# Gate's low parts of the first chunk: from GpSimd to VectorE

## The chip, the core and the metric

The kernel runs on one core of a Trainium2 chip. The metric is the time of one execution on the device in microseconds (us). The engines are TensorE (PE in the profile), VectorE (DVE), ScalarE (ACT), GpSimd (POOL) and the queue engine SyncE (SP). Each works through its own instructions in order and waits on semaphores for the others.

## What is computed

Attention in which a query sees the first `n_sink` (4) keys and the `window` (128) keys that end at itself, for 4 batches of 8 heads, 768 positions and head width 64; then, on the 3072 tokens of width 512 that result, a gated layer with a hidden width of 1536:

```
scores = scale * q @ k.T, outside window and sinks -1e9
a = exp(scores - max);  a = a / (sum(a) + 1e-9)
x = (a @ v), heads joined: 3072 x 512
out = ((x @ w_a) * (x @ w_b)) @ w_out
```

## The kernel before

**Tiling.** The tokens are taken in eight chunks (`CHUNKS`): the first has four tiles of 128 tokens, the second two, the others three. For each chunk `moe` runs over j = 0 to 11, the twelve slices of 128 of the hidden width. `half("a", j)` and `half("b", j)` are twelve matmuls each (L813), ScalarE brings a out of PSUM as g (L832), VectorE multiplies b into it (L838), and `project` multiplies the slice by its part of `w_out` (L822), one j later than the slice was made. In the first chunk these tiles are 512 columns wide.

**Split numbers.** Every matmul of this part is three matmuls of float16: each value is a high part and a low part, and low times low is left out. For g the high part gh is a cast on ScalarE (L841). The low part gl is g minus gh (L843), a subtraction of two operands in SBUF. It is done on GpSimd for j = 0 to 9 and on VectorE for j = 10 and 11. g has a single buffer, so that the next j's g (L832) waits until gh and gl of this j are taken; gh and gl have two each.

**Weights.** They come as 64-bit words and are converted once, during the first chunk: `weight_bits` (L352, L354 on VectorE and L353 on ScalarE), `weight_sum` (L361, VectorE), `weight_high` (L367, ScalarE), `weight_low` (L372, VectorE). From the seventh on two weights are converted by one instruction of each kind. The order of the weights is that of their use: w_a and w_b of slice j, then w_out of slice j - 2.

**Attention beside it.** While `moe` works on one chunk, `between` advances the attention of the next by some steps. In the first chunk this attention rounds its keys and queries on ScalarE (L401) and takes their rest on VectorE (L407), not on GpSimd; all its score tiles go through one PSUM bank `s`. A score tile (L530, PE) is read by VectorE (L540), which frees the bank for the next; then come exp (L542, ACT), two small operations (L544, L545, DVE), the division (L553, ACT) and a transpose (L578, PE). At a group's end the sinks' part is added to x (L605 on PE, L607 on VectorE).

**What sets the order.** A scheduler places each engine's instructions by priorities and by its own idea of when they become ready, except where `keep_in_program_order` binds them (the conversions are bound among themselves). L843 is not bound. `run` makes the chunks one after the other and calls `moe`.

Of the kernel before, what the change touches and what calls it, by code (L numbers as in the profile page):

```python
# [18 lines left out]
B, H, S, D = 4, 8, 768, 64  # L19
DM, FF = 512, 1536  # L20
P = 128
# [3 lines left out]
NJ = FF // P  # L25
# [207 lines left out]
class Fast:  # L233
# [562 lines left out]
            xs.append((xh, xl))  # L796
        return xs

    def moe(self, row, nt, xf, between, weights_ahead, last):
        nc = self.nc  # L800
        n = nt * P
        tag = f"{row}"
        xs = self.split_x(xf, nt, tag)
        outs = [self.ps.tile([P, DM], F32, tag=("o0", "o1", "o2", "av")[i], name=f"o{tag}_{i}") for i in range(nt)]

        def half(kind, j):
            wh, wl = self.weight(kind, j)
            ps = self.ps.tile([P, 4 * P], F32, tag=kind, name=f"{kind}{tag}_{j}")
            for kk in range(NK):
                ksl = slice(kk * P, (kk + 1) * P)  # L810
                xh, xl = xs[kk]
                for i, (w, x) in enumerate(((wh, xh), (wh, xl), (wl, xh))):
                    nc.tensor.matmul(ps[:, :n], lhsT=w[:, ksl], rhs=x[:, :n],  # L813
                                     start=kk == 0 and i == 0, stop=kk == NK - 1 and i == 2)
            return ps

        def project(j, gh, gl):
            wh, wl = self.weight("o", j)
            for i in range(nt):
                sl = slice(i * P, (i + 1) * P)  # L820
                for k, (g, w) in enumerate(((gh, wh), (gh, wl), (gl, wh))):
                    nc.tensor.matmul(outs[i], lhsT=g[:, sl], rhs=w,  # L822
                                     start=j == 0 and k == 0, stop=j == NJ - 1 and k == 2)

        prev = None
        for j in range(NJ):
            if last and j == NJ - 2:
                self.good = self.verdict()
            weights_ahead(3 * j)
            pa = half("a", j)  # L830
            g = self.mo.tile([P, max(n, 3 * P)], F32, tag="g", name=f"g{tag}_{j}", bufs=1)
            nc.scalar.activation(g[:, :n], pa[:, :n], AF.Copy, scale=G_UP / (X_UP * W_UP) ** 2)  # L832
            between(3 * j)
            if last and j == NJ - 1:
                self.tc.mark_branch_hint_location("general", hint="LikelyTaken", engines=mybir.ALL_ENGINES)
            weights_ahead(3 * j + 1)
            pb = half("b", j)
            nc.vector.tensor_tensor(g[:, :n], pb[:, :n], g[:, :n], op=ALU.mult)  # L838
            gh = self.mo.tile([P, max(n, 3 * P)], F16, tag="gh", name=f"gh{tag}_{j}")
            gl = self.mo.tile([P, max(n, 3 * P)], F16, tag="gl", name=f"gl{tag}_{j}")  # L840
            nc.scalar.copy(gh[:, :n], g[:, :n])  # L841
            e = nc.gpsimd if j < NJ - 2 else nc.vector
            e.tensor_tensor(gl[:, :n], g[:, :n], gh[:, :n], op=ALU.subtract)  # L843
            between(3 * j + 1)
            weights_ahead(3 * j + 2)
            if prev is not None:
                project(*prev)
            between(3 * j + 2)
            if j >= 2 and self.unsummed:
                o, k = self.unsummed.pop(0)  # L850
                self.sum_rows(o, o, k)
            prev = (j, gh, gl)
        project(*prev)
        down = 1.0 / (G_UP * W_UP)
        scalar = lambda o, ps: nc.scalar.activation(o, ps, AF.Copy, scale=down)
        vector = lambda o, ps: nc.vector.tensor_scalar(o, ps, down, None, op0=ALU.mult)
        os = [self.mo.tile([P, DM], F32, tag="os", name=f"os{tag}_{i}", bufs=4) for i in range(nt)]
        if not last:
            for i in range(nt):
                r = row + i * P  # L860
                scalar(os[i], outs[i])
                nc.scalar.dma_start(self.out[r:r + P, :], os[i])
                self.unsummed.append((os[i], r // P))
            return
        pin = self.tc.keep_in_program_order
        for i in range(nt):
            r = row + i * P
            if i == nt - 1:
                for c, (e, q) in enumerate(((scalar, nc.sync), (vector, nc.scalar))):
                    sl = slice(c * (DM // 2), (c + 1) * (DM // 2))  # L870
                    pin(e(os[i][:, sl], outs[i][:, sl]))
                    pin(q.dma_start(self.out[r:r + P, sl], os[i][:, sl]))
                continue
            pin(scalar(os[i], outs[i]))
            nc.sync.dma_start(self.out[r:r + P, :], os[i])
            if i == 0:
                pin(self.sum_rows(outs[i], os[i], r // P, down))
        for i in range(1, nt):
            sums = self.rows[:, row // P + i:row // P + i + 1]
            if i == nt - 1:  # L880
                pin(self.sum_rows(outs[i], os[i], row // P + i, down))
            else:
                pin(nc.scalar.activation(outs[i], outs[i], AF.Square, scale=down, accum_out=sums))
# [10 lines left out]
    def run(self, scalars, verdict, whole):  # L894
        chunks = CHUNKS
# [4 lines left out]
        def weights_to(n, ahead):  # L900
            wide = range(SINGLE, 2 * PAIRS)
            while loaded[0] < min(n + ahead, len(order)):
                if loaded[0] >= len(order) - 4 and done[0] <= 2 * PAIRS:
                    break
                self.load_weight(loaded[0])
                loaded[0] += 1
            while done[0] < min(n + DELAY, len(order) + DELAY):
                k = done[0]
                done[0] += 1
                singles = lambda d: 0 <= k - d < len(order) and k - d not in wide  # L910
                if singles(3):
                    self.weight_low(k - 3, 1)
                if k % 2 == 0 and k - 2 in wide:
                    self.weight_low(k - 2, 2)
                if singles(2):
                    self.weight_high(k - 2, 1)
                if singles(1):
                    self.weight_sum(k - 1, 1)
                if k % 2 == 1 and k - 1 in wide:
                    self.weight_sum(k - 1, 2)  # L920
                    self.weight_high(k - 1, 2)
                if singles(0):
                    self.weight_bits(k, 1)
                if k % 2 == 0 and k in wide:
                    self.weight_bits(k, 2)
# [5 lines left out]
        b, t0, nt = chunks[0]  # L931

        x = self.wp.tile([P, NK, nt * P], F32, tag=f"w{3 * NJ // 2 - 1}", name="xf0")
        xf = [x[:, i, :] for i in range(NK)]
# [12 lines left out]
        for c, (b, t0, nt) in enumerate(chunks):  # L947
            gen = None
            if c + 1 < len(chunks):
                nb, nt0, nnt = chunks[c + 1]  # L950
                nxf = self.new_xf(c + 1)

                self.banks = ("t", "o2") if nt == 2 else ("t",)
                gen = (self.attention if c else self.attention_in_one_bank)(nb, nt0, nnt, nxf)
                steps = H * nnt + (6 if c else 7)
            taken = [0]

            def between(s):
                if gen is None:
                    return  # L960
                if c == 1 and s == 0:
                    self.join_masks()
                if c:
                    want = min(steps, -(-steps * (s + 1) // (3 * NJ - 3)))
                else:
                    n = HALF * nnt + 2
                    want = 1 if s < BEGIN else max(-(-n * (s + 1 - QUIET) // (MID - QUIET)), 2)
                    if s >= MID:
                        want = min(steps, n - (n - steps) * (s + 1 - MID) // (3 * NJ - 3 - MID))
                while taken[0] < want:  # L970
                    next(gen, None)
                    taken[0] += 1

            def ahead(s):
                weights_to(max(s + AHEAD, done[0] + 1 - DELAY), LOADS)
                if (c, s) in checks:
                    self.check_weight(*order[checks.index((c, s))])
                elif self.unchecked:
                    self.check_weight(None, 0)

            self.moe(b * S + t0 * P, nt, xf, between, ahead, c + 1 == len(chunks))
            if gen is not None:
                for _ in gen:
                    pass
                xf = nxf
# [76 lines left out]
```

## Time and profile before

| | |
|---|---|
| three runs | 731.34, 732.73, 732.94 us, median 732.73 |
| the profiled execution | 734.26 us |
| its span in the profile | 732.5 us |
| TensorE busy in the span | 715.1 us (98%), granted clock 0.999 |
| VectorE, ScalarE, GpSimd busy | 438.2 (60%), 384.5 (52%), 257.6 us (35%) |

The span begins with the first instruction and ends with the last; the 1.8 us between it and the execution's time lie around it. TensorE's 98% are an average: the first 40 us hold the attention of the first chunk, the stretch from about 40 to 160 us its `moe` with the conversion of the weights, and the rest the other seven chunks. An engine's idle time counts only where the time of the whole hangs on it.

### The profile page before, as it was taken

How to read it: one execution, taken by the hardware profiler on the slowest of the kernel's cores; microseconds unless marked ns; L12 is line 12 of the kernel's file. 1: busy time of each engine (PE TensorE's matmuls, PEld its weight loads, DVE VectorE, ACT ScalarE, POOL GpSimd, SP SyncE). 2: the span in 40 equal slices, each digit the busy share in tenths (PEclk: the TensorE clock that was granted, in tenths of full speed). 3: DMA queues.
4: the chain of work that ended last, by engine and by line, in shares of the span. 5: the costliest groups of instructions: out<-in, count | busy, mean ns of one | idle time of the engine just before them, and what ended most of it. 6: DMA issues, size and time to landing. Idle time of an engine off the chain costs nothing.

```text
span 732.5 us, 13093 instructions
## 1 busy us (share of the span) xinstructions
PE 715.1 (98%) x4400; PEld 426.5 (58%) x4400; DVE 438.2 (60%) x1496; ACT 384.5 (52%) x1107; POOL 257.6 (35%) x324
## 2 busy tenths in 40 slices
PE   9999899999999999999999999999999999999996
PEld 4644444457776666566665666556665666655553
DVE  5999999985535665364534555345655545436632
ACT  4957877746655554355543655355553555441112
POOL 1311110356642553254641655225434454101110
PEclk9999999999999999999999999999999999999999
DMA  8988200342221442411221111113333122016411
GB/s 289 345 293 306 68 14 1 108 142 56 63 76 44 123 129 88 141 52 48 62 63 55 46 53 42 65 58 110 105 124 113 59 63 73 4 61 210 155 51 46
DMA packets 43527, 73.35 MB, mean 100 GB/s; under 512 B 4608, under 2 KB 24128, under 8 KB 43456
## 3 DMA queue, kind: packets, MB, share of 16 engines
q1 hardware_dynamic: 40064, 66.70, 28.4%
q10 hardware_dynamic: 3392, 5.77, 2.1%
q8 instruction: 36, 0.59, 0.3%
q14 instruction: 35, 0.29, 0.1%
HBM read 66.16 MB, written 6.29 MB: 99 GB/s over the span
## 4 chain that ended last, share of the span: by engine, by line
PE 83%; DVE 11%; ACT 3%; issue 2%; DMA 0%; ACTq 0%; DVEq 0%
PE o L822 22%; PE b L813 22%; PE a L813 22%; PE s L530 5%; PE av L468 4%; PE t L572 2%; DVE wf L361 2%; DVE w L372 2%; DVE wf L352 2%; DVE wf L354 2%; DVE g L838 1%; PE t L679 1%; PE t L578 1%; PE s_a L644 1%; DVE p L540 1%
## 5 line engine op out<-in xcount | busy, mean ns | idle before, releaser
L813 PEld LDWEIGHTS <-w 128*128 128x128 f16 x2304 | 224.1, 98 | 136.8 <-DVE w L372 0.7
L813 PE MATMUL b<-x,w 128*128 128x384 f16 (+2 forms) x1152 | 205.9, 326 | 0.0
L813 PE MATMUL a<-x,w 128*128 128x384 f16 (+2 forms) x1152 | 205.5, 326 | 0.0
L843 POOL TENSOR_TENSOR gl<-g,gh 128x384 f16<-128x384 f32 (+2 forms) x80 | 76.0, 950 | 301.6 <-ACT gh L841 297.6
L822 PE MATMUL o<-w,gh 128*128 128x512 f16 x576 | 171.8, 379 | 0.7 <-DVE w L372 0.7
L822 PE MATMUL o<-w,gl 128*128 128x512 f16 x288 | 109.0, 379 | 0.1
L841 ACT CAST gh<-g 128x384 f16<-128x384 f32 (+2 forms) x96 | 49.0, 510 | 100.9 <-DVE g L838 98.6
L542 ACT ACTIVATE p<-p,st 128x136 f32<-128x136 f32 (+1 forms) x160 | 66.6, 416 | 52.9 <-DVE st L540 52.1
L838 DVE TENSOR_TENSOR g<-b,g 128x384 f32<-128x384 f32 (+2 forms) x96 | 53.3, 555 | 68.5 <-PE b L813 61.5
L822 PEld LDWEIGHTS <-gh 128*128 128x128 f16 x576 | 55.4, 98 | 51.6 <-ACT gh L841 1.9
L832 ACT ACTIVATE g<-a 128x384 f32<-128x384 f32 (+2 forms) x96 | 46.3, 482 | 68.4 <-PE a L813 59.3
L530 PE MATMUL s<-ks,qh 128*128 128x264 f32 x160 | 66.9, 418 | 5.0 <-DVE st L540 4.6
L550 ACT ACTIVATE p<-p,st 128x128 f32<-128x128 f32 x120 | 48.2, 401 | 40.8 <-DVE st L545 40.6
L544 DVE TENSOR_SCALAR st<-st 128x1 f32<-128x1 f32 x160 | 24.3, 152 | 65.3 <-ACT p L542 64.7
L538 DVE COPY_PREDICATED s<-mg,s 128x128 f32<-128x128 int32 x120 | 35.0, 292 | 41.8 <-PE s L530 41.7
L409 POOL TENSOR_TENSOR ks<-kr,ks 64x400 fp32r<-64x400 f32 (+1 forms) x48 | 56.6, 1178 | 3.8
L403 POOL TENSOR_SCALAR qh<-qr 128x384 fp32r<-128x384 f32 x48 | 24.9, 518 | 83.6 <-PE s L530 66.9
L573 DVE TENSOR_TENSOR pt<-t,tri 128x256 f32<-128x256 f32 x120 | 50.3, 419 | 3.6 <-PE t L572 2.9
L822 PEld LDWEIGHTS <-gl 128*128 128x128 f16 x288 | 28.1, 98 | 36.5 <-DVE gl L843 2.6
L409 POOL TENSOR_TENSOR ql<-qr,qh 128x384 fp32r<-128x384 f32 x48 | 48.6, 1012 | 2.2
L530 PE MATMUL s<-ks,ql 128*128 128x264 f32 x160 | 45.3, 283 | 0.0
L530 PEld LDWEIGHTS s<-ks,qh 128*128 128x128 f32 x160 | 30.3, 189 | 23.7 <-DVE st L540 9.1
(146 smaller groups left out, 902.2 us busy)
## 6 DMA issues: line engine op xcount, KB each, us to landing
qr<-in_qT_dram SPq DMA_DIRECT2D x48, 192.0 KB, 2.4
raw<-in_wa_dram SPq DMA_DIRECT2D x12, 512.0 KB, 6.0
raw<-in_wb_dram SPq DMA_DIRECT2D x12, 512.0 KB, 6.2
raw<-in_wo_dram SPq DMA_DIRECT2D x12, 512.0 KB, 6.9
chk_a<-in_wa_dram SPq DMA_DIRECT2D x24, 256.0 KB, 3.4
chk_b<-in_wb_dram SPq DMA_DIRECT2D x24, 256.0 KB, 3.4
chk_o<-in_wo_dram SPq DMA_DIRECT2D x24, 256.0 KB, 3.3
out_dram<-os ACTq DMA_DIRECT2D x21, 256.0 KB, 2.2
```

The costliest lines, as they stand in the source:

```text
L409: self.nc.gpsimd.tensor_tensor(o, i, high.bitcast(F32), op=ALU.subtract)
L530: mm = nc.tensor.matmul(ps[:, :w], lhsT=q[:, i * P:(i + 1) * P], rhs=ks[:, c0:c0 + w], start=m == 0, stop=m == 1)
L538: nc.vector.copy_predicated(ps[:, KB:], self.up, ps[:, :P])
L542: nc.scalar.activation(p[:, :w], p[:, :w], AF.Exp, bias=st[:, 0:1], scale=-1.0, accum_out=st[:, 1:2])
L550: nc.scalar.mul(p[:, NS:KB], p[:, NS:KB], st[:, 3:4])
L573: nc.vector.tensor_tensor(pt[:, k:k + 2, :], tp[:, 0:1, :].broadcast_to([P, 2, P]), self.tri, op=ALU.mult)
L813: nc.tensor.matmul(ps[:, :n], lhsT=w[:, ksl], rhs=x[:, :n], start=kk == 0 and i == 0, stop=kk == NK - 1 and i == 2)
L822: nc.tensor.matmul(outs[i], lhsT=g[:, sl], rhs=w, start=j == 0 and k == 0, stop=j == NJ - 1 and k == 2)
L832: nc.scalar.activation(g[:, :n], pa[:, :n], AF.Copy, scale=G_UP / (X_UP * W_UP) ** 2)
L838: nc.vector.tensor_tensor(g[:, :n], pb[:, :n], g[:, :n], op=ALU.mult)
L841: nc.scalar.copy(gh[:, :n], g[:, :n])
L843: e.tensor_tensor(gl[:, :n], g[:, :n], gh[:, :n], op=ALU.subtract)
```

## The change

`moe` gets one more argument. It is false for chunk 0 and true for all others, and where it is false gl is taken on VectorE for every j. Ten subtractions of 128x512 go from GpSimd's queue to VectorE's; nothing else is computed in another place.

```
-    def moe(self, row, nt, xf, between, weights_ahead, last):
+    def moe(self, row, nt, xf, between, weights_ahead, last, weights_split):
...
-            e = nc.gpsimd if j < NJ - 2 else nc.vector
+            e = nc.gpsimd if weights_split and j < NJ - 2 else nc.vector
             e.tensor_tensor(gl[:, :n], g[:, :n], gh[:, :n], op=ALU.subtract)
...
-            self.moe(b * S + t0 * P, nt, xf, between, ahead, c + 1 == len(chunks))
+            self.moe(b * S + t0 * P, nt, xf, between, ahead, c + 1 == len(chunks), c > 0)
```

The scheduler also sets other instructions of the first chunk in another order. From the second chunk on the order of all engines is as it was. Three places follow; in a name the number after `g`, `gh` or `gl` is j, and in `p_4_2_0` the numbers are the first tile (4), the head (2) and the tile within (0) of the attention that runs beside.

**Place 1.** VectorE after g of slice 4, before:

```order
L838 TENSOR_TENSOR g_4_979<-b_4_1001,g_4_979 128x512
L407 TENSOR_TENSOR ks_3_4_1021<-kr_2_4_916,ks_3_4_1021 64x400
L372 SCALAR_TENSOR_TENSOR w_896<-wf,w_896 128x1024
L540 ISA p_4_2_0_1031,st_4_2_0_1032<-s_4_2_0_1028,mg 128x264
L540 ISA st_4_2_0_1032 128x1
L352 TENSOR_SCALAR wf<-raw_705 128x1024
```

and now:

```order
L838 TENSOR_TENSOR g_4_979<-b_4_1001,g_4_979 128x512
L407 TENSOR_TENSOR ql_3_4_1023<-qr_3_4_1019,qh_3_4_1022 128x256
L540 ISA p_4_2_0_1031,st_4_2_0_1032<-s_4_2_0_1028,mg 128x264
L540 ISA st_4_2_0_1032 128x1
L372 SCALAR_TENSOR_TENSOR w_896<-wf,w_896 128x1024
L843 TENSOR_TENSOR gl_4_1016<-g_4_979,gh_4_1015 128x512
L352 TENSOR_SCALAR wf<-raw_705 128x1024
```

gl_4 stands three operations behind g_4, and the reading of the score tile (L540) has moved ahead of the conversion L372 and of the rest of the keys ks_3.

**Place 2.** VectorE before the scores of head 6, before:

```order
L407 TENSOR_TENSOR ks_7_4_1380<-kr_6_4_1281,ks_7_4_1380 64x400
L372 SCALAR_TENSOR_TENSOR w_1267<-wf,w_1267 128x1024
L407 TENSOR_TENSOR ql_7_4_1382<-qr_7_4_1378,qh_7_4_1381 128x256
L352 TENSOR_SCALAR wf<-raw_995 128x1024
L540 ISA p_4_6_0_1390,st_4_6_0_1391<-s_4_6_0_1387,mg 128x264
```

and now:

```order
L843 TENSOR_TENSOR gl_7_1375<-g_7_1339,gh_7_1374 128x512
L361 ISA wf<-raw_944,wf 128x2048
L407 TENSOR_TENSOR ks_7_4_1380<-kr_6_4_1281,ks_7_4_1380 64x400
L407 TENSOR_TENSOR ql_7_4_1382<-qr_7_4_1378,qh_7_4_1381 128x256
L540 ISA p_4_6_0_1390,st_4_6_0_1391<-s_4_6_0_1387,mg 128x264
L540 ISA st_4_6_0_1391 128x1
L372 SCALAR_TENSOR_TENSOR w_1267<-wf,w_1267 128x1024
```

Here too L540 now stands ahead of L372, and of L352.

**Place 3.** The sinks' part of the second group, near the end of the first chunk. VectorE before:

```order
L352 TENSOR_SCALAR wf_1597<-raw_1437 128x512
L354 SCALAR_TENSOR_TENSOR wf_1597<-raw_1437,wf_1597 128x512
L372 SCALAR_TENSOR_TENSOR w_1594<-wf_1543,w_1594 128x512
L361 ISA wf_1597<-raw_1437,wf_1597 128x1024
L352 TENSOR_SCALAR wf_1630<-raw_1437 128x512
L607 TENSOR_TENSOR xf_2_620<-t_4_0_0_940,xf_2_620 128x256
```

and now:

```order
L352 TENSOR_SCALAR wf_1597<-raw_1437 128x512
L607 TENSOR_TENSOR xf_2_620<-t_4_0_0_940,xf_2_620 128x256
L354 SCALAR_TENSOR_TENSOR wf_1597<-raw_1437,wf_1597 128x512
L372 SCALAR_TENSOR_TENSOR w_1594<-wf_1543,w_1594 128x512
L361 ISA wf_1597<-raw_1437,wf_1597 128x1024
```

TensorE there, before and then now:

```order
L813 MATMUL a_10_1634<-x_3_631,w_1481 128x512
L605 MATMUL t_4_0_0_940<-sct_4_1_1623,vs_4_4_1108 128x256
L813 LDWEIGHTS w_1540
L813 MATMUL b_10_1655<-x_0_622,w_1540 128x512
```

```order
L813 MATMUL b_10_1655<-x_2_628,w_1540 128x512
L605 MATMUL t_4_0_0_940<-sct_4_1_1623,vs_4_4_1108 128x256
L813 LDWEIGHTS w_1540
L813 MATMUL b_10_1655<-x_2_628,w_1540 128x512
```

The addition L607 has moved ahead of four conversions, and the matmul L605 that it reads from stands eight matmuls later; the second L605, which needs L607's bank, still follows all twelve matmuls of b_10.

## Rows read from the trace of the kernel before

**Rows 1.** Stretches: busy us (instructions) of each engine, clock, DMA share, GB/s.
```profile
0.00:40.00 40.00, 38.49 (x272) 22.60 (x274) 31.02 (x117) 27.42 (x85) 9.51 (x26) 1.00 0.93 324
40.00:160.00 120.00, 110.90 (x573) 53.85 (x570) 113.48 (x199) 83.99 (x183) 25.99 (x23) 1.00 0.36 121
160.00:733.00 573.00, 565.75 (x3561) 350.08 (x3559) 293.75 (x1182) 273.11 (x841) 222.11 (x275) 1.00 0.26 80
```

**Rows 2.** Waits of TensorE, 40 to 160 us: total us, times, longest.
```profile
PE s L530 <- DVE st L540: 4.4, 4, 1.6
PE t L605 <- DVE xf L607: 1.6, 1, 1.6
PE t L578 <- ACT xf L586: 1.4, 2, 1.2
PE o L822 <- DVE w L372: 0.7, 1, 0.7
PE t L578 <- ACT pt L579: 0.6, 1, 0.6
```

**Rows 3.** Waits of TensorE from 160 us to the end.
```profile
PE gp L90 <- DVE good L88: 2.8, 1, 2.8
```

**Rows 4.** GpSimd's timeline, first and last gl: start, duration, [idle before <-releaser].
```profile
47.94 1.48 POOL L843 TENSOR_TENSOR gl<-g,gh 128x512 f16<-128x512 f32 x1 [10.93 <-ACT gh L841]
...
139.59 2.39 POOL L843 TENSOR_TENSOR gl<-g,gh 128x512 f16<-128x512 f32 x1 [9.20 <-ACT gh L841]
143.25 1.65 POOL L403 TENSOR_SCALAR ks<-kr 64x400 fp32r<-64x400 f32 x2 [1.27 <-DMA kr<-in_kT_dram]
```

**Rows 5.** VectorE's timeline, one operation (L361) beside these two, and alone.
```profile
48.32 1.65 DVE L361 CUSTOM_DVE_ANT_0 wf<-raw,wf 128x1024 uint16<-128x1024 uint16 x1
...
131.29 0.69 DVE L361 CUSTOM_DVE_ANT_0 wf<-raw,wf 128x1024 uint16<-128x1024 uint16 x1
...
141.44 1.09 DVE L361 CUSTOM_DVE_ANT_0 wf<-raw,wf 128x1024 uint16<-128x1024 uint16 x1
```

**Rows 6.** VectorE's timeline, gl of slices 10 and 11, and the operation behind.
```profile
151.91 0.98 DVE L843 TENSOR_TENSOR gl<-g,gh 128x512 f16<-128x512 f32 x1
...
156.64 0.69 DVE L843 TENSOR_TENSOR gl<-g,gh 128x512 f16<-128x512 f32 x1 [0.68 <-ACT gh L841]
157.25 1.62 DVE L792 SCALAR_TENSOR_TENSOR x<-xf,x 128x256 f16<-128x256 f32 x4
```

**Rows 7.** TensorE's timeline, four of its waits.
```profile
84.76 0.39 PE L530 MATMUL s<-ks,qh 128*128 128x264 f32 x1 [0.89 <-DVE st L540]
...
108.16 0.44 PE L578 MATMUL t<-ident,p 128*128 128x128 f32 x2 [1.20 <-ACT xf L586]
...
121.70 0.39 PE L530 MATMUL s<-ks,qh 128*128 128x264 f32 x1 [0.93 <-DVE st L540]
...
146.99 0.38 PE L605 MATMUL t<-sct,vs 128*128 128x256 f32 x1 [1.59 <-DVE xf L607]
```

**Rows 8.** ScalarE's timeline, the division ahead of L586.
```profile
107.33 0.52 ACT L553 ACTIVATE p<-p,st 128x264 f32<-128x264 f32 x1 [1.75 <-DVE st L545]
```

**Rows 9.** Groups of VectorE, 46 to 150 us: busy us, mean ns | idle before.
```profile
L372 DVE SCALAR_TENSOR_TENSOR w<-wf,w 128x1024 f16<-128x1024 f32 x11 | 13.4, 1223 | 1.4 <-ACT w L367 1.2
```

**Rows 10.** Timelines of VectorE and ScalarE, g and gh of slices 0 and 9.
```profile
46.51 0.69 DVE L838 TENSOR_TENSOR g<-b,g 128x512 f32<-128x512 f32 x1
47.24 0.62 ACT L841 CAST gh<-g 128x512 f16<-128x512 f32 x1 [1.06 <-DVE g L838]
...
136.94 0.68 DVE L838 TENSOR_TENSOR g<-b,g 128x512 f32<-128x512 f32 x1
138.91 0.60 ACT L841 CAST gh<-g 128x512 f16<-128x512 f32 x1
```

**Rows 11.** The last conversion of a weight (VectorE), and its first use (TensorE).
```profile
152.82 1.48 DVE L372 SCALAR_TENSOR_TENSOR w<-wf,w 128x512 f16<-128x512 f32 x1
157.59 0.59 PE L822 MATMUL o<-w,gh 128*128 128x512 f16 x2
```

## The prediction

> **What bounds the kernel now.** I read the stretches first. From 160 us to the end TensorE is busy 565.75 of the 572.5 us that are left of the span [rows 1], and the only wait of note there is the final check, 2.8 us [rows 3]; the order of these chunks is unchanged, so they should take what they took. The first 40 us hold no gl. What is open is the stretch from 40 to 160 us: TensorE is busy 110.90 of 120 us, so it loses 9.1 us, while VectorE is busy 113.48 of 120 us [rows 1]. The waits say the same from the other side: 4.4 us for the PSUM bank of the scores that VectorE must first read (L540), 1.6 us for L607 on VectorE, 0.7 us for a converted weight, and 2.0 us for ScalarE's copies [rows 2]. In this stretch VectorE is the engine that is late, and 9.1 us is the most that any change here can give back.
>
> **What the change removes.** While GpSimd takes a gl, an operation of VectorE that should begin stands still. The first gl runs from 47.94 to 49.42 [rows 4]; VectorE's L361 begins at 48.32 and takes 1.65 us, where the same operation alone takes 0.69 [rows 5]: 0.96 us lost. The tenth gl holds VectorE less, 1.09 against 0.69 us, 0.40 us [rows 5], and is held up itself, 2.39 us [rows 4]. I found one such operation at each of the ten gl and took its excess over its like beside no GpSimd work: 7.9 us for the ten, from 0.40 to 0.97 us each.
>
> That trace fits a rule of the Trainium skill, "SBUF — State Buffer", section "Who interferes with whom": GpSimd and VectorE share one pair of ports, and where both read SBUF through it, VectorE with two operands as here, whichever comes second is blocked until the first has finished. By that rule the loss would be the whole rest of GpSimd's operation, 49.42 - 48.32 = 1.10 us for the first [rows 4, 5] where its stretching shows 0.96; over ten some 9.3 instead of 7.9 us, and VectorE's balance below would be -3.2 instead of -1.8 us. I take the stretching, which is measured.
>
> **What it adds.** Ten subtractions on VectorE. gl of slices 10 and 11 show the price at this very width: 0.69 us undisturbed, 0.61 us from its start to the next start, and 0.98 us where GpSimd runs beside it [rows 6]. Beside nine of the ten GpSimd will have nothing to do (its next work, the keys of a later chunk, begins at 143.25 [rows 4]), so I take 0.61: 6.1 us for ten, with 9.8 us as the upper end. VectorE's balance is 6.1 - 7.9 = -1.8 us, and +1.9 us at the upper end.
>
> A second rule speaks against the change: "Perfetto Trace Analysis", section "Optimizing Scalar/DVE Operations", says that where VectorE is saturated, offloading work to ScalarE or GpSimd may make sense, though between VectorE and GpSimd it might not help. VectorE is saturated here, so by the first half the move is the wrong way and the 6.1 us come on top; this is a rival below. The stretched operations [rows 5] bear out the second half.
>
> **What it adds as a wait.** gl now stands in VectorE's queue and needs gh from ScalarE; behind it stand conversions, L540 and L607, and behind those TensorE. From the end of g to the end of gh it took 47.86 - 47.20 = 0.66 us at slice 0 and 139.51 - 137.62 = 1.89 us at slice 9 [rows 10], over the ten 13.4 us. The new order puts other work between g and gl: at place 1 a subtraction, L540 and L372, of which L372 alone is 1.22 us [rows 9]. Only for the last three slices is the work between about as short as the lag or a little shorter (at slice 9 two short conversions against 1.89 us). Bounds: nothing, or 1.2 us if ScalarE kept its old order; it takes gh_9 earlier now, so I count nothing.
>
> **Which waits of TensorE go.** VectorE gaining 1.8 us would by itself bring about 1.8 us. But TensorE waits at single points, and the new order moves them too. In order of time:
> - 0.7 us for a weight [rows 2]: the first stall (0.96) is gone and one gl (0.61) stands ahead of it, so 0.35 us.
> - The four waits for the bank make 4.4 us [rows 2]. In the first (1.6 us) L540 falls behind more of VectorE's work than before and I give it nothing. By the second four stalls (3.6 us) have been exchanged for four gl (2.4 us); VectorE is 1.2 us ahead, so TensorE is at most 1.2 us ahead in all. At place 1 L540 passes L372, 1.22 us [rows 9], and the 0.89 us [rows 7] go: 2.1 us so far.
> - 1.20 us behind L586 on ScalarE [rows 7]: L586 queues behind L553, which waits 1.75 us for VectorE's L545 [rows 8], late by a stall. ScalarE now has L586 first. I count 0.5 of it, since the weights then lie close: 2.6 us.
> - 0.93 us at head 6 [rows 7]: at place 2 L540 passes L372 and L352. 0.85 us: about 3.4 us.
> - 1.59 us at L605 [rows 7]: at place 3 L607 passes four conversions, and TensorE has eight matmuls to do before the first L605. All of it: 5.0 us.
>
> The end of the chunk sets a limit of its own: the last weight is ready at 154.30, its matmuls begin at 157.59 [rows 11], 3.3 us later; with VectorE 1.8 us ahead TensorE can be 5.1 us ahead and no more.
>
> So the ends are 1.8 us (VectorE's balance alone) and 5.0 us (every new place pays). Which it is cannot be read from before, as ScalarE is also busy 83.99 of 120 us [rows 1] in its own new order; new small waits are likely. I take the middle, 3.4 us. The profiled execution of 734.26 us would be 730.9; it lies 1.5 us over the median of 732.73, and the same 3.4 us off the median make 729.3 us.
>
> **Rivals.**
> - *No difference.* VectorE gets ahead, but the waits only move: in the new order two readings of score tiles follow each other directly, so VectorE itself waits for TensorE between them, and conversions fall behind where L540 passes them. For it: the exchange is worth only 1.8 us in all. Against: the weights have 3.3 us to spare at the end [rows 11]. A gain of 0 to 1.4 us: about 732.
> - *Slower: VectorE stands at gl for gh.* The place is L843 in VectorE's queue. If ScalarE, with 70% of its time taken [rows 1], brings gh 0.6 us late each time, VectorE loses 6.0 us against the 1.8 won: +4.2 us, 736.9 us. It turns the sign at a mean wait of 0.18 us and is slower by a measurable amount from 0.33 us. Against: the work placed between g and gl.
> - *Slower: relief taken from a saturated engine.* The 6.1 us come on top and the stalls do not come back, because VectorE would have stood there for other reasons. Less the 3.3 us to spare that is +2.8 us, 735.5 us. Against: behind the stretched operations VectorE goes on without idling.
> - *More than forecast.* If the bank waits vanish altogether, up to 6 us: 726.7.
>
> **How the numbers follow.** A measurement of this kernel can tell about 0.2% (1.5 us) from no change, so faster means under 731.3 and slower over 734.2. Forecast (1.8 to 5.0 us off: 727.7 to 730.9) 0.62, more than that 0.06, no difference 0.21, slower by the wait for gh 0.08, by the load 0.03. Faster 0.68, same 0.21, slower 0.11. The range goes from 727.0, a little beyond the forecast's end, to 733.8, which takes in most of the no-difference case.
>
> **What would show it.** VectorE's operations of the first chunk without stretched ones until GpSimd starts on the keys; ten gl on VectorE near 0.69 us, no idle time before them for ACT gh; TensorE's idle time from 40 to 160 us down from 9.1 to about 5.7 us, above all no wait at L605; after that the chunks as long as before. Idle time at gl of over 2 us in all, or TensorE losing more than 8 us in this stretch, would make the prediction wrong.

## The result and the profile after

The changed kernel takes 725.6 us in the median of four runs (724.88 to 726.1) against 732.84 us of the kernel before (731.34 to 734.97). The ratio is 0.9898, with a 95% interval from 0.9872 to 0.9925: 7.2 us less. Forecast were 729.3 us with a range from 727.0 to 733.8, so the direction was right, but the gain is about twice what I expected and lies outside the range.

The stretches of the changed kernel, to be held against [rows 1]. The columns are busy us (instructions) of PE, PE's weight loads, DVE, ACT and POOL, then clock, DMA share, GB/s:

```profile
0.00:40.00 40.00, 38.11 (x300) 22.97 (x301) 33.43 (x121) 28.66 (x88) 9.51 (x26) 1.00 0.95 336
40.00:160.00 120.00, 116.37 (x607) 58.64 (x606) 113.00 (x235) 87.11 (x198) 14.88 (x19) 1.00 0.38 127
160.00:725.00 565.00, 557.11 (x3496) 343.55 (x3494) 287.20 (x1151) 267.84 (x822) 217.82 (x270) 1.00 0.26 79
```

From 40 to 160 us TensorE now loses 3.6 us instead of 9.1. But TensorE also issued 300 matmuls in the first 40 us where it had issued 272, in a stretch without any gl. The fixed windows thus mix two things. A better ruler lies inside the program: the twelve g of the first chunk (L838). Here are the first and the last of them on the timeline of VectorE in the changed kernel:

```profile
43.15 0.69 DVE L838 TENSOR_TENSOR g<-b,g 128x512 f32<-128x512 f32 x1
...
146.82 0.68 DVE L838 TENSOR_TENSOR g<-b,g 128x512 f32<-128x512 f32 x1
```

and the last one of the kernel before, whose first stands in [rows 10] at 46.51:

```profile
155.27 0.69 DVE L838 TENSOR_TENSOR g<-b,g 128x512 f32<-128x512 f32 x1 [0.97 <-PE b L813]
```

This cuts both executions into three. Up to the first g: 46.51 and 43.15 us, 3.36 less. From the first to the last: 108.76 and 103.67, 5.09 less. From there to the end of the span: 577.2 and 577.2. The sum, 8.45 us, is the difference of the two profiled executions, 734.26 - 725.81. So the first chunk gave 5.1 us, the later chunks nothing, and 3.4 us come from a place that the change does not touch.

This ruler is VectorE's. In the kernel before, the last g waited for the last matmul of b_11 and began 0.1 us behind it, as the first g does in both kernels. In the changed kernel these matmuls (the first line here) end at 145.37 us, and the last g begins 1.4 us later, because VectorE is still busy:

```profile
142.62 2.75 PE L813 MATMUL b<-x,w 128*128 128x512 f16 x12
...
155.54 0.39 PE L530 MATMUL s<-ks,qh 128*128 128x264 f32 x1 [0.60 <-DVE st L540]
```

TensorE was thus 6.4 us ahead at this point and gave 1.2 us back behind it, 0.46 at L822 and 0.60 at the L530 shown, both while waiting for VectorE. In the changed kernel VectorE is still the late engine at the end of the chunk.

What VectorE did between these two g, in the kernel before and then in the changed one (columns as above):

```profile
46.50:155.28 108.78, 99.68 (x506) 48.58 (x505) 104.55 (x182) 77.91 (x172) 24.53 (x21) 1.00 0.33 106
```

```profile
43.14:146.83 103.69, 100.66 (x509) 48.97 (x508) 100.96 (x192) 77.89 (x172) 9.19 (x11) 1.00 0.34 114
```

VectorE has exactly ten instructions more (192 against 182), the ten gl, and is busy 3.6 us less. Its idle time fell too, from 4.2 to 2.7 us. 3.6 and 1.5 make the 5.1 us.

The remaining waits of TensorE from 40 to 160 us (total us, times, longest), to be held against [rows 2]:

```profile
PE s L530 <- DVE st L540: 1.9, 2, 1.3
PE o L822 <- DVE w L372: 0.7, 2, 0.5
PE a L813 <- ACT w L367: 0.3, 1, 0.3
PE t L605 <- ACT sct L598: 0.3, 1, 0.3
```

The bank's waits went from 4.4 to 1.9 us (1.25 us in the first chunk, and the new 0.60 us shown above), the 1.59 us at L605 behind L607 is gone, and the 1.2 us behind L586 have no successor. Half of a microsecond at L822 is new, and so are 0.3 us each at L813 and, behind ScalarE, at L605. Of the 9.1 us of waits before, 7.6 us went, and 1.7 us of new ones came. The difference, 5.9 us, is more than the chunk's 5.1, since TensorE also idles 0.4 us longer in pieces too short for this list and loses 0.2 us more at an L530 behind 160 us.

On GpSimd nothing meets VectorE until late; its timeline begins, after the start, with

```profile
119.87 0.24 POOL L292 IOTA col<- 128x128 f32 x1 [86.22 <-PE t L578]
135.47 1.74 POOL L403 TENSOR_SCALAR ks<-kr 64x400 fp32r<-64x400 f32 x2 [15.36 <-DVE sct L597]
```

and VectorE's timeline around its first gl, to be held against the stretched L361 of [rows 5], reads

```profile
44.96 0.69 DVE L361 CUSTOM_DVE_ANT_0 wf<-raw,wf 128x1024 uint16<-128x1024 uint16 x1
45.56 0.69 DVE L352 TENSOR_SCALAR wf<-raw 128x1024 int32<-128x1024 int32 x1
46.17 0.69 DVE L843 TENSOR_TENSOR gl<-g,gh 128x512 f16<-128x512 f32 x1
46.77 1.22 DVE L354 SCALAR_TENSOR_TENSOR wf<-raw,wf 128x1024 int32<-128x1024 int32 x1
```

L361 takes 0.69 us where it took 1.65, gl 0.69 us and 0.60 to the next start, and no idle time stands in front of it.

### The profile page after: what moved, and what is told of

It reads as the page before. It is cut to its first block, busy times and chain, and to the rows that moved or that the text cites. A ratio compares the mean times of both kernels' runs of the same rounds, so it can differ in the third digit from the quotient of the medians.

```text
span 724.0 us, 13079 instructions
## 1 busy us (share of the span) xinstructions
PE 711.6 (98%) x4400; PEld 425.2 (59%) x4400; DVE 433.6 (60%) x1506; ACT 383.6 (53%) x1107; POOL 242.2 (33%) x314
## 4 chain that ended last, share of the span: by engine, by line
PE 78%; DVE 11%; DMA 5%; ACT 3%; issue 2%; SPq 0%; ACTq 0%; DVEq 0%
PE o L822 22%; PE b L813 21%; PE a L813 21%; PE s L530 5%; PE av L468 4%; DMA raw<-in_wa_dram 3%; PE t L572 2%; DVE wf L354 2%; DVE wf L361 2%; DVE w L372 2%; DVE wf L352 1%; DMA out_dram<-os 1%; DVE gl L843 1%; DVE g L838 1%; ACT w L367 1%
## 5 line engine op out<-in xcount | busy, mean ns | idle before, releaser
L813 PEld LDWEIGHTS <-w 128*128 128x128 f16 x2304 | 223.8, 98 | 139.0 <-DVE w L372 1.8
L813 PE MATMUL b<-x,w 128*128 128x384 f16 (+2 forms) x1152 | 206.8, 326 | 0.3
L813 PE MATMUL a<-x,w 128*128 128x384 f16 (+2 forms) x1152 | 205.3, 326 | 0.3 <-ACT w L367 0.3
L822 PE MATMUL o<-w,gh 128*128 128x512 f16 x576 | 172.7, 379 | 0.7 <-DVE w L372 0.7
L843 POOL TENSOR_TENSOR gl<-g,gh 128x384 f16<-128x384 f32 (+1 forms) x70 | 61.7, 882 | 211.6 <-ACT gh L841 208.1
L822 PE MATMUL o<-w,gl 128*128 128x512 f16 x288 | 109.0, 379 | 0.1
L838 DVE TENSOR_TENSOR g<-b,g 128x384 f32<-128x384 f32 (+2 forms) x96 | 53.3, 555 | 68.3 <-PE b L813 60.8
L822 PEld LDWEIGHTS <-gh 128*128 128x128 f16 x576 | 55.5, 98 | 51.7 <-ACT gh L841 1.9
L832 ACT ACTIVATE g<-a 128x384 f32<-128x384 f32 (+2 forms) x96 | 46.3, 482 | 70.6 <-PE a L813 64.5
L530 PE MATMUL s<-ks,qh 128*128 128x264 f32 x160 | 67.1, 419 | 2.3 <-DVE st L540 2.2
L822 PEld LDWEIGHTS <-gl 128*128 128x128 f16 x288 | 28.1, 98 | 36.3 <-DVE gl L843 3.0
L530 PE MATMUL s<-ks,ql 128*128 128x264 f32 x160 | 45.3, 283 | 0.0
L530 PEld LDWEIGHTS s<-ks,qh 128*128 128x128 f32 x160 | 30.3, 190 | 19.6 <-DVE st L540 4.8
```

The lines of the kernel that those rows point to most:

```text
L530: mm = nc.tensor.matmul(ps[:, :w], lhsT=q[:, i * P:(i + 1) * P], rhs=ks[:, c0:c0 + w], start=m == 0, stop=m == 1)
L813: nc.tensor.matmul(ps[:, :n], lhsT=w[:, ksl], rhs=x[:, :n], start=kk == 0 and i == 0, stop=kk == NK - 1 and i == 2)
L822: nc.tensor.matmul(outs[i], lhsT=g[:, sl], rhs=w, start=j == 0 and k == 0, stop=j == NJ - 1 and k == 2)
```

## The experiments

Two theories of the 5.1 us. **P**: GpSimd's reading of g and gh held VectorE back, and the change takes that away. **O**: the reading hardly matters; the ten gl in VectorE's queue made the scheduler put L540, L607 and L586 earlier, and that new order made the gain. For the 3.4 us at the start there are two more: the change moves them, or they differ from execution to execution of any kernel.

### Both kernels again

e1_before_again and e2_after_again are the two kernels without an edit, on one chip with e3 and e4.

> The kernel before, unchanged, once more. In its profile TensorE's first matmuls came at the lower of its two rates until 12.4 us (a fill matmul of 512 columns every 0.43 us), in the profile of the changed kernel only until 5.0 us (every 0.22 us); the changed kernel was 3.4 us ahead before any instruction differed. Theory A (chance): when the rate rises differs from execution to execution in both kernels; then the times spread over some 3.5 us, from 731 to 735 us, and this profile may show either rate. Theory B (it belongs to the kernel): all times near 733 us, and the profile again shows 0.43 us until about 12 us. Either way the ratio to the kernel before is 1.000 within 0.003.

> The changed kernel, unchanged, once more. Theory A: times spread from 724.5 to 729 us, the ratio settles at 0.993 (5.1 us, the gain that the two profiles show between the first product g of the first chunk and the last), and the rest of the 7.2 us was luck. Theory B: all times at 725 to 726 us, ratio 0.990, and the profile shows the higher rate from 5 us on.

Before: 731.81 us (730.68 to 733.51, 12 runs). After: 725.47 us (725.17 to 728.99, 5 runs), ratio to before 0.9903 [0.9878, 0.9928]. The result repeats, with the ratio that theory B of e2 had, not the 0.993 of theory A. The kernel before was timed in a second set on the same chip: these 23 runs have a median of 733.28 us (731.15 to 736.76), and e1 stands to them at a ratio of 0.9978 [0.9964, 0.9993]. Medians of one program thus differ by 1.5 us here, and a difference of that size is not read as an effect. VectorE's timeline in this run of the kernel before has the first and the last g at

```profile
42.90 0.69 DVE L838 TENSOR_TENSOR g<-b,g 128x512 f32<-128x512 f32 x1
...
151.62 0.69 DVE L838 TENSOR_TENSOR g<-b,g 128x512 f32<-128x512 f32 x1 [0.97 <-PE b L813]
```

108.72 us apart, as in the first profile (108.76), but with the first g 3.6 us earlier. The kernel before can therefore start early without the change, as theory A of e1 had it. In e2 the two are 103.81 us apart.

### The new order, with GpSimd's reading put back

e3_dummy_on_gpsimd is the changed kernel, in which GpSimd subtracts beside each of the ten, into a tile that nobody reads:

```
             e.tensor_tensor(gl[:, :n], g[:, :n], gh[:, :n], op=ALU.subtract)
+            if not weights_split and j < NJ - 2:
+                spare = self.mo.tile([P, 4 * P], F16, tag="spare", name=f"spare{j}", bufs=1)
+                nc.gpsimd.tensor_tensor(spare[:, :n], g[:, :n], gh[:, :n], op=ALU.subtract)
```

> The changed kernel, with ten extra subtractions g - gh on GpSimd in the first chunk, into a tile that nobody reads. The order of TensorE, VectorE and ScalarE is that of the changed kernel, row for row; only GpSimd's reading comes back. Theory P (GpSimd's reading holds VectorE): ten operations of VectorE are stretched again by 0.4 to 1.0 us each, about 7.9 us in all, and with the 6.1 us of the ten gl that stay on VectorE the first chunk gets as long as in the kernel before or longer: 730 to 734 us. Theory O (the new order of the queues made the gain): under 1 us more than the changed kernel, 725 to 727 us.

735.14 us (734.04 to 738.39, 12 runs), ratio to before 1.0033 [1.0018, 1.0047]. That is a little beyond the 730 to 734 us that theory P had, and 9.7 us above the median of e2, though the instructions of TensorE, VectorE and ScalarE stand in the same order as in e2. GpSimd's first two extra subtractions, on its timeline,

```profile
44.40 1.48 POOL L846 TENSOR_TENSOR spare<-g,gh 128x512 f16<-128x512 f32 x1 [10.92 <-ACT gh L841]
53.21 1.40 POOL L846 TENSOR_TENSOR spare<-g,gh 128x512 f16<-128x512 f32 x1 [7.33 <-ACT gh L841]
```

and what VectorE does at these times:

```profile
44.79 1.65 DVE L361 CUSTOM_DVE_ANT_0 wf<-raw,wf 128x1024 uint16<-128x1024 uint16 x1
...
53.50 1.66 DVE L843 TENSOR_TENSOR gl<-g,gh 128x512 f16<-128x512 f32 x1
```

The same L361 as above is back at 1.65 us, and the second gl takes 1.66 instead of 0.69. Between first and last g (columns as for the stretches):

```profile
42.97:155.84 112.87, 101.36 (x509) 48.65 (x508) 109.89 (x192) 78.35 (x172) 28.07 (x21) 1.00 0.32 105
```

VectorE is busy 8.9 us longer than in the changed kernel with the same 192 instructions, and the first chunk is 9.2 us longer. Followed instruction by instruction against the changed kernel, the ten that lie beside GpSimd's ten take 0.84 to 0.97 us more nine times and 0.39 us once, 8.9 us together. The extra subtraction also keeps g's single buffer taken for longer, and ScalarE's L832 waits 2.5 us for it once; but VectorE's idle time between the two g hardly grows (3.0 us against 2.7 in the changed kernel), so the price lies in the stretched operations. P holds. O falls as the cause of the gain: with the new order and the reading together the chunk is 4.1 us longer than in the kernel before. VectorE's busy time is 5.3 us longer than there (109.89 against 104.55), so something over 1 us may be left for the order.

### The old order, without GpSimd's reading

e4_before_without_reading is the kernel before, with gl of slices 0 to 9 of the first chunk set to zero by GpSimd instead of computed:

```
-            e.tensor_tensor(gl[:, :n], g[:, :n], gh[:, :n], op=ALU.subtract)
+            if not weights_split and j < NJ - 2:
+                nc.gpsimd.memset(gl[:, :n], 0.0)
+            else:
+                e = nc.gpsimd if j < NJ - 2 else nc.vector
+                e.tensor_tensor(gl[:, :n], g[:, :n], gh[:, :n], op=ALU.subtract)
```

> The kernel before, but in the first chunk, for slices 0 to 9, GpSimd fills gl with zeros and does not compute it, so it reads nothing. The order of TensorE, VectorE and ScalarE is that of the kernel before, row for row, and VectorE has no gl to take. Theory P: the ten stretched operations are gone, VectorE is up to 7.9 us ahead, TensorE's idle time between 40 and 160 us falls from 9.1 to 3 to 5 us, and the time is 727 to 729 us with the old order. Theory O: in the old order TensorE still waits at the same places, 731 to 733 us.

723.91 us (723.25 to 724.8, 4 runs), ratio 0.9875 [0.9853, 0.9898], with TensorE, VectorE and ScalarE in the order of the kernel before. That is 3 us below the 727 to 729 us of theory P; TensorE loses 2.5 us from 40 to 160 us, where 3 to 5 were expected. Between first and last g:

```profile
42.84:143.94 101.10, 99.04 (x506) 48.78 (x505) 95.52 (x182) 77.61 (x172) 14.93 (x19) 1.00 0.36 124
```

VectorE is busy 9.0 us less than before with the same 182 instructions, and the chunk is 7.7 us shorter. GpSimd still writes each gl, as on its timeline

```profile
50.63 0.52 POOL L843 MEMSET gl<- 128x512 f16 x1 [15.63 <-PE o L822]
```

and no operation of VectorE is stretched before the keys come at 133 us. What held VectorE was the operation that reads two tiles, not the writing of gl. P again: without a change of order the first chunk gives back about what the stalls had cost.

The three places of the new order can be looked up here as well. In the old order the wait at place 1 stays as it was, 0.89 us, as on TensorE's timeline

```profile
77.83 0.39 PE L530 MATMUL s<-ks,qh 128*128 128x264 f32 x1 [0.89 <-DVE st L540]
```

while the 0.93 us at head 6 are gone and of the 1.59 us at L605 only 0.15 are left, without the new order of places 2 and 3. In the changed kernel all three are gone. But VectorE has less work in e4 than there, and no run has the old order with gl on VectorE; what the new order adds to the gain is therefore not shown.

Beside this kernel the price of gl on VectorE can be read. The changed kernel has 5.4 us more of VectorE's work (100.96 against 95.52) but its chunk is only 2.6 us longer. The difference went into VectorE's idle time, 5.6 us here and 2.7 there. The waits of VectorE in this stretch, first of e4, then of the changed kernel:

```profile
DVE w L372 <- ACT w L367: 2.5, 3, 1.2
DVE g L838 <- PE b L813: 1.6, 2, 1.4
```

```profile
DVE p L540 <- PE s L530: 1.0, 2, 0.6
DVE w L372 <- ACT w L367: 0.5, 1, 0.5
```

Some of the gl thus stand where VectorE would have waited for ScalarE or TensorE. How much of this is the gl filling gaps and how much the other order of the rest, these runs do not separate.

### Half of the slices

e7_first_five_slices takes gl of slices 0 to 4 on VectorE, e11_last_five_slices that of slices 5 to 9, both from the changed kernel:

```
-            e = nc.gpsimd if weights_split and j < NJ - 2 else nc.vector
+            e = nc.gpsimd if (weights_split or j >= 5) and j < NJ - 2 else nc.vector
```

(`j < 5` in e11).

> Only slices 0 to 4 of the first chunk take gl on VectorE, slices 5 to 9 on GpSimd. The stalls that go make 4.2 us, the five gl that come 3.1 us. Theory P: about half the gain, 728 to 731 us; five operations of VectorE are still stretched, at slices 5 to 9. Rival (the gain arises only late in the chunk, where TensorE waited 1.6 us at L605): at most 1 us, 732 us.

> The other half: slices 5 to 9 of the first chunk take gl on VectorE, slices 0 to 4 on GpSimd. Slices 0 to 4 alone on VectorE gave 728.3 us, 4.3 us less than before. The stalls that go here make 3.7 us, the gl that come 3.1 us. Theory P alone, by the balance: a little less than that half, 729 to 731 us. If the two halves add up to the whole of 7.1 us: 729.5 to 730 us. Rival (the order's lottery, each order has its own waits): anywhere from 725 to 733 us.

e7: 728.3 us (727.78 to 728.46), ratio 0.9947 [0.9933, 0.9961]; first to last g 106.11 us, 2.6 less than before. e11: 727.93 us (726.68 to 729.96), ratio 0.994 [0.9918, 0.9961]; 105.08 us, 3.7 less. VectorE has five stretched operations in each, beside the five gl that GpSimd still takes, and none of the kind beside the others. Each half gains, as P wants, e11 a little more than the 729 to 731 us that were expected; but together they make 6.3 us where the whole makes 5.0. The halves are not additive: each has an order of its own and, in e7, new waits of TensorE, such as 1.4 us for ScalarE's copy of the probabilities (L579) and 1.0 us at L593 for L540.

### The start

In the kernel before, as first profiled, the first g comes at 46.5 us, in e1 at 42.9. On TensorE's timeline the fill matmuls (L650, 512 columns each, put among the first scores) show why. The kernel before:

```profile
9.03 1.04 PE L650 MATMUL fill<-z 128*128 128x512 bf16 x2
...
11.18 1.46 PE L650 MATMUL fill<-z 128*128 128x512 bf16 x3
```

The same kernel in e1:

```profile
6.89 0.60 PE L650 MATMUL fill<-z 128*128 128x512 bf16 x2
...
8.32 0.82 PE L650 MATMUL fill<-z 128*128 128x512 bf16 x3
```

One more matmul in the group adds 0.42 us in the one and 0.22 us in the other: 512 columns at the level of 1.2 GHz, or of 2.4 GHz. The granted clock column shows 1.00 for these first 40 us in both. Both begin alike, with eight warming matmuls that take 3.59 us up to 4.93 or 4.94 us. In the first profile the low level then lasts until about 12.4 us, in e1 until 5 to 6 us.

Three more executions of the kernel before, with a profile and no edit:

> The kernel before once more, one look at its start. Theory A: the fill matmuls come every 0.43 us until some point between 5 and 13 us that differs from both executions seen so far, or like one of them; the stretch from the first g to the last takes 108.7 us as in both. Theory C: that stretch differs by over 1 us.

> The kernel before, one more look. The times of this kernel go from 730.7 to 736.8 us, those of the changed one, but for a single execution, from 724.9 to 726.1. Each look is cut at the first and the last g of the first chunk. Theory A (the start): only the part up to the first g varies, 42.9 to 46.5 us. Theory C (the first chunk): the part between the two g varies around 108.7 us by over 1 us. Theory D (later): the part after the last g varies around 577.3 us by over 1 us.

> As the look before, of another execution: theory A up to the first g, 42.9 to 46.5 us; theory C between the first g and the last, otherwise 108.7 us; theory D after the last g, otherwise 577.3 us.

| execution | first g | first to last g | last g to the end | time |
|---|---|---|---|---|
| before, first profile | 46.51 | 108.76 | 577.2 | 734.26 |
| e1 | 42.90 | 108.72 | 577.3 | 730.68 |
| e8 | 42.95 | 108.74 | 577.4 | 730.81 |
| e9 | 43.08 | 108.79 | 577.4 | 731.0 |
| e10 | 46.42 | 108.78 | 577.1 | 734.13 |
| after, first profile | 43.15 | 103.67 | 577.2 | 725.81 |
| e2 | 42.87 | 103.81 | 577.5 | 725.9 |

So the kernel before was profiled three times with an early start and twice with a late one, some 3.5 us apart, and everything behind it takes the same time to within 0.3 us: theory A holds, C and D fall. With the same start the change is worth 5.0 us (730.83 in the mean of three against 725.86 in the mean of two), all of it in the first chunk. These two starts are not all of the spread: of 72 recorded times of the kernel before, eight lie above 734.5 us, up to 736.76, beyond what either profiled start gives.

Can a longer warm-up at the very start fix the level? e5_before_longer_warm and e6_after_longer_warm:

```
-WARM = 8
+WARM = 12
```

> The kernel before with 12 instead of 8 warming matmuls at its start. In two executions of the kernel before, TensorE's rate rose at 12.4 us in one (span 732.5 us) and before 6 us in the other (span 728.9 us). Theory A (the start is chance, and the spread of the times comes from it): with four more matmuls TensorE is still at work when the rate rises, the rate is high before the attention begins in every execution, and the times draw together to within 1.5 us, at 730 to 732.5 us (the longer warming can cost up to 1.7 us). Theory C (the spread of the kernel before comes from the first chunk, where GpSimd and VectorE collide): the spread stays at 3 to 5 us.

> The changed kernel with 12 warming matmuls. Theory A: against the kernel before with 12 the difference is what the change does in the first chunk alone, 4.7 to 5.1 us: 725 to 727.5 us. Theory C: the difference to the kernel before with 12 stays at 6 to 7 us.

e5: 734.22 us (732.61 to 735.91, 11 runs), ratio to before 1.0021 [1.0006, 1.0036]. e6: 726.09 us (725.29 to 726.49, 5 runs), ratio 0.9918 [0.9905, 0.9932]. The spread of the kernel before did not narrow to theory A's 1.5 us: it is 3.3 us. Its profile has an early start (first g at 43.11) but a longer first chunk (109.85) and 1.3 us more behind it, 733.71 us in all, so a long time need not mean a late start; with the four matmuls some operations of ScalarE and VectorE had come into another order too. The two kernels with 12 differ by 8.1 us, more than either theory had, though both profiles start early (43.11 and 43.38): 6.0 us of it lie in the first chunk. The attempt failed and does not say what sets the level.

### The second chunk too

e12_two_chunks was to be a better version: the second chunk's gl goes to VectorE as well.

```
-            self.moe(b * S + t0 * P, nt, xf, between, ahead, c + 1 == len(chunks), c > 0)
+            self.moe(b * S + t0 * P, nt, xf, between, ahead, c + 1 == len(chunks), c > 1)
```

> The changed kernel with gl on VectorE in the second chunk as well (ten more subtractions, 256 columns wide). In the second chunk TensorE hardly waits, so theory P gives no difference to the changed kernel, 725 to 726.5 us; if the waits of up to 0.9 us for L540 after 155 us come from GpSimd's reading, up to 1 us less, 724.5 us; if VectorE gets late by the ten, 727 us.

729.04 us (726.12 to 731.8, 12 runs), ratio to before 0.996 [0.9941, 0.9978]: not better than the changed kernel, and slower than each of the three expectations. In its profile the first chunk is as long as there (44.91 to 148.69, 103.78 us), the start 1.8 us later, the time from the last g to the end of the span 579.6 instead of 577.2 us, and TensorE has new waits from 160 us to the end, the two longest of which are:

```profile
PE s L530 <- DVE st L545: 0.8, 1, 0.8
PE s L530 <- DVE st L540: 0.6, 1, 0.6
```

Its times spread over 5.7 us; where the unprofiled ones differ was not seen.

## Why the prediction was wrong

- **VectorE is the late engine from 40 to 160 us.** Right. Taking 9.0 us from it (e4) shortens the chunk by 7.7 us, giving it 8.9 us more (e3) lengthens it by 9.2 us.
- **The stalls, 7.9 us.** Right in kind and size: against the same ten operations in e4 they are 7.9 us, and none is left before GpSimd's first keys. e3 and e4 show them as the cause. My condition that VectorE's operation has two operands was too narrow: three of the ten are L352, which reads one tile, and they were held for 0.61 to 0.97 us like the others.
- **Ten gl at 0.61 us, 6.1 us.** Right: they take 0.60 us each from start to start.
- **The balance, -1.8 us.** The first step that failed, by its size: it is -3.6 us. Stalls and gl together were right (6.0 - 7.9 = -1.9). But I had left out that the keys' work on GpSimd, which also stretches VectorE [rows 4, 6], would fall otherwise: counted in the same way, it cost VectorE 4.3 us before (143 us to the last g) and 3.4 us after (from 135 us), -0.9 us. For the last 0.8 us I found no single operation. The rule of the Trainium skill that I weighed ("SBUF — State Buffer", section "Who interferes with whom") came to -3.2, nearer in sum, though not by its path: in e3 GpSimd ends at 45.88, 1.09 us after L361's start at 44.79, and L361 is 0.96 us longer.
- **gh is ready in time.** Right: at none of the ten gl does VectorE idle for it. At slice 11, which VectorE took before too, it idles 0.69 us where it was 0.68 [rows 6].
- **Which waits of TensorE go: 3.4 us, the middle of 1.8 and 5.0.** This sum failed with the balance; measured are 5.0 us at the same start. The seven waits that I had counted at 5.0 us gave back 6.4 us, and four others that I had given nothing (0.63 us behind L579 and three of 0.2) went too: 7.6 us. My discount of 1.6 us for new small waits was about right, as 1.7 us of them came (0.46 at L822, 0.34 at L813, 0.32 at L605, 0.60 at L530). What it was taken from was too small. The likely reason is the balance: I held TensorE to VectorE's lead, and VectorE was 3.6 us ahead in all, not 1.8; the lower end was that balance itself. That the measured 5.0 us equal my upper end is luck, more waits gone less the new ones. So is their agreement with the limit of 5.1 us from the weights' lead [rows 11]: it was worked out with the same 1.8 us and would be 6.9 with 3.6. Two waits that I gave little or nothing only shrank, the weight's from 0.69 to 0.20 us and the first for the bank from 1.58 to 1.25:

```profile
64.12 0.39 PE L530 MATMUL s<-ks,qh 128*128 128x264 f32 x1 [1.25 <-DVE st L540]
...
135.93 0.38 PE L605 MATMUL t<-sct,vs 128*128 128x256 f32 x1 [0.32 <-ACT sct L598]
...
146.05 0.38 PE L822 MATMUL o<-w,gh 128*128 128x512 f16 x1 [0.46 <-DVE w L372]
```

  These are three of TensorE's waits in the changed kernel: one old one that is left, and two of the new. The 1.59 us at L605 [rows 7] did go, but 0.32 us behind ScalarE stand there now.
- **The first 40 us, put at nothing because they hold no gl.** The second step that failed. No instruction there changed, but its time is not one number: some 3.5 us lie between the two starts of the kernel before. Its recorded median, 732.73, lies between the two kinds (730.8 and 734.2 in profiles), and I took its start over into the forecast. The changed kernel ran with the early start in both of its profiles, and eight of nine recorded times, 724.88 to 726.1, fit that start. Against the gain of 5.0 us at the same start, 2.2 of the 7.2 us are left, and the starts would account for them; this is not shown, since the level in the unprofiled runs was not seen. Why the kernel before so often starts late or in between, and whether the change has a hand in it, stays open. The profiles only show that the same program does both.
- **The later chunks.** Right: 577.2 us from the last g to the end, before and after. Counted on TensorE, from the last matmul of b_11 to its last one, it is 1.2 us longer in the changed kernel.
- **The rivals.** No difference, the wait for gh and the load on a saturated engine all fell. So did the advice that I had set against the change ("Perfetto Trace Analysis" of the Trainium skill, section "Optimizing Scalar/DVE Operations", to offload a saturated VectorE): taking 6.0 us of work back from GpSimd onto it shortened VectorE's busy time. Its second half, that between the two it might not help, fits. "More than forecast" came nearest with 726.7 us, but by a mechanism that did not occur: the bank's waits did not vanish, 1.9 us of them are left.

## What to carry to other kernels

An operation that GpSimd takes over need not be free for VectorE: here each two-operand subtraction on GpSimd cost VectorE 0.79 us in the mean, 0.40 to 0.97, more than the 0.60 us of doing it itself; look for stretched operations beside GpSimd's before counting an offload as relief. Where the low end, the price of each wait and the limit are all worked out from one balance, their agreement proves nothing: here the balance was half of the truth, and all three were too small with it. Before a gain of 1% is forecast or explained, cut several profiles of the same kernel at a fixed instruction: the part that varies by itself is then seen, and does not end up on the change's account.

## What was not expected of the hardware

- Executions of one program differ in how long TensorE stays at the lower of its two levels at the start (until 12.4 us, or until 5 to 6 us), which puts them some 3.5 us apart, with the granted clock shown as 1.00 both times. In e11 and e12 it lies between: low until about 10 us, first g at 44.84 and 44.91 us.
- GpSimd's writing alone (a 128x512 memset, 0.52 us) held VectorE nowhere in e4; two of the ten memsets were themselves longer, 0.71 and 0.91 us, each beside an L352 of VectorE. GpSimd's reading of two tiles held VectorE at all ten places in e3.
- One program, timed in two sets on one chip, gave medians of 731.81 and 733.28 us.
